# Token sums kept in spent raw tokens, an early ring, earlier weight sums and wider attention steps in an attention + MoE-style FFN kernel

## The chip, the cores and the metric

The kernel runs on one NeuronCore of one Trainium2 chip. Its engines work side by side, each with its own queue of instructions: TensorE (PE in the profile, PEld for its weight loads), VectorE (DVE), ScalarE (ACT), GpSimd (POOL) and SyncE (SP), which here issues all DMAs. The metric is the time of one execution in device microseconds (us).

## The reference

Windowed attention over 8 batches, 8 heads, 576 positions, head size 64, in fp32, and a feed-forward layer on its output. Heads 0 to 3 look back 32 positions, heads 4 to 7 look back 128 positions in steps of 4.

```python
scores = scale * q @ k.T                         # per batch and head
scores = np.where(mask, scores, -1e9); attn = softmax(scores); x = attn @ v
x = x.transpose(0, 2, 1, 3).reshape(4608, 512)   # tokens x d_model
h = x @ w_in                                     # 512 -> 2048
g = np.maximum(h, 0) + alpha * np.minimum(h, 0)
return g @ w_out                                 # 2048 -> 512
```

## The kernel before, in words

Every fp32 matrix is split into a high part (rounded to the fast fp32r type by ScalarE) and a low part (the rest, subtracted by VectorE). A product is three passes: high x high, high x low, low x high.

*Attention* works on 32 pairs of heads (class `Pair`; pair p is batch p // 4, heads 2c and 2c + 1 with c = p % 4). A pair has these steps: `scores` (72 small matmuls, L192), `maxima` (VectorE adds the mask and takes row maxima from PSUM, L216), `exponentials` (ScalarE, L228), `divisions` (VectorE, L235 to L238), `transposes` (TensorE, L248), `copies` (ScalarE, L255), `values` (72 small matmuls, L266), `highs` (ScalarE, L302) and `lows` (VectorE, L307 and L309), which put the result into token tiles. Tokens of the first three tiles of 512 go to split `x` tiles, later ones to unsplit *raw* tiles (`raw_xA0`, `raw_xB0`, `raw_xB1`, which share buffers with spent `x` tiles).

*The feed-forward layer* has two phases. In the first, three token tiles go through 48 *slices*, each one tile times 128 of the 2048 hidden columns: `ffn_h` (12 matmuls, L375), the activation (`ffn_sum`, or `ffn_parts` on VectorE, L396 and L397), `ffn_high` (ScalarE, L402), `ffn_low` (VectorE, L407), `ffn_y` (12 matmuls, L422). Slice n issues h of slice n + 1 and y of slice n - 1. The order of slices is tile 0's first eight, tile 1's sixteen, tile 0's last eight (24 to 31), tile 2's (32 to 47). When tile 0 resumes, its first partial output is loaded back from DRAM (`part`, L420) and added (L430).

The second phase (`paired_stage`) takes tiles 3 to 8 two at a time, in three stages with a Strassen-like scheme: seven products (`B11`, `B21`, `B22`, `T1` to `T4`) instead of eight. It needs sums of tokens (`token_parts`: T1 = z0 - k0, T2 = z1 - T1, T3 = z1 - z0, T4 = k1 - T2, where k0, k1 are the halves of the even raw tile, z0, z1 of the odd one) and sums of weights. Weights are saved to DRAM during slices 24 to 39 (`save`); in the last sixteen slices GpSimd forms sums for eight pairs of weight columns (`combine`, L465 and L468), ScalarE and VectorE split them (`split_combined`, L473 and L474), and they go to DRAM too. The stage reads all weights through a ring of ten buffers (`slot`, `take`, `feed`, L508).

Each stage has two groups; a group is an h part (`phase_h`, products of L561) and a y part (`phase_y`, L699) of four columns with eight *units* of six matmuls. Work of other kinds is hung on units by number (`hooks`): the steps of 12 attention pairs (`attention_hooks`: begin = scores, maxima, exponentials; middle = divisions, transposes, copies; end = values, highs, lows), and the token sums of the next stage. At the end of a column its result is copied to `py` (L717, L719) or added to it and stored (L722, L723).

The order on every engine is the program's order: the schedule is written out by hand (`manual_schedule`), and an engine that waits holds everything behind it. `score_at`, `turn_at`, `value_at` and `divide_at` say in which slice a pair takes its steps; `late_ops` holds the token sums of the first stage. `const.tile` with a tag that is in use waits until the earlier tile's readers are done. PSUM's four `a` banks are handed out in turn to h, scores, transposes and values.

Of the kernel before, what the change touches and what calls it, by code (L numbers as in the profile page):

```python
# [9 lines left out]
F32 = mybir.dt.float32  # L10
# [5 lines left out]
P = 128  # L16
# [17 lines left out]
EARLY = 21  # L34
# [23 lines left out]
def tile_window_attention_prelu_ffn(  # L58
# [381 lines left out]
    WBLOCK = {1: 0, 2: 1, 4: 2, 5: 3, 6: 4, 7: 5, 3: 6}  # L440
# [17 lines left out]
    def combine(i):  # L458

        if "t" not in sums_at:  # L460
            sums_at["t"] = const.tile([P, 8, 2 * P], F32, tag="xA1", name="wsum")
        t = sums_at["t"]
# [4 lines left out]
        for out, x, y, op in ((4, 2, 3, ALU.add), (5, 4, 0, ALU.subtract), (6, 0, 2, ALU.subtract), (7, 1, 5, ALU.subtract)):  # L467
            nc.gpsimd.tensor_tensor(out=t[:, out], in0=t[:, x], in1=t[:, y], op=op)  # L468

    def split_combined(i):  # L470
        t = sums_at["t"][:, 4:]
        hi, lo = (gbuf([P, 4, 2 * P], F32R, f"wc{i}_{a}") for a in range(2))
        nc.scalar.copy(out=hi, in_=t)  # L473
        nc.vector.tensor_tensor(out=lo, in0=t, in1=hi.bitcast(F32), op=ALU.subtract)  # L474
        for a, w in enumerate((hi, lo)):
            nc.sync.dma_start(out=wS[i, 3:7, :, a].rearrange("q p n -> p q n"), in_=w.bitcast(F32))

# [55 lines left out]
    def token_parts(t, tmp):  # L533
# [3 lines left out]
        T1, T2, T3, T4 = tmp  # L537
# [7 lines left out]
        def low(name, x):  # L545
# [4 lines left out]
        first = [diff(T1, z0, k0), high("T1", T1), low("T1", T1)]  # L550
        second = [
            diff(T2, z1, T1), high("T2", T2), diff(T3, z1, z0), high("T3", T3), low("T2", T2), low("T3", T3),
            diff(T4, k1, T2), high("B22", z1), high("T4", T4), low("B22", z1), low("T4", T4),
# [133 lines left out]
    def phase_y(t, grp, u, hooks):  # L687

        end = grp + 1 == NFP // GP
        for c in range(NC):  # L690
# [23 lines left out]
            for tt in range(2):  # L714
# [8 lines left out]
                nc.sync.dma_start(out=outT[c * P:(c + 1) * P, (t + tt) * TT:(t + tt + 1) * TT], in_=o)  # L723

    def attention_hooks(hooks, us, start, step):
        def put(n, *ops):
            hooks.setdefault(n, []).extend(ops)

        for k, u in enumerate(us):
# [24 lines left out]
            put(n + step + 1, end)  # L754

    def paired_stage():
# [3 lines left out]
        for t in range(NSTD, NTILE, 2):  # L760
            for grp in range(NFP // GP):
# [6 lines left out]
                attention_hooks(hooks, us, 2, 5)  # L768
                if grp and t + 2 < NTILE:
                    lots = token_parts(t + 2, [temporary(i) for i in range(1, 5)])  # L770
                    for at, lot in zip((4, 10, 20) if t == NSTD else (4, 10, 16), lots):
# [4 lines left out]
    held = {}  # L776

    def hold(i):
        if i not in held:
            held[i] = const.tile([P, 2 * TT], F32, tag=f"w{2 + i}_1", name=f"hold{i}")  # L780
        return held[i]

# [318 lines left out]
```

## Time and profile before

| | |
|---|---|
| time, median of 3 runs | 934.85 us (930.09 to 935.88) |
| profiled execution | 930.15 us; its span 928.4 us, granted TensorE clock 0.979 |
| busy time | PE 871.6 (94%), VectorE 554.2 (60%), ScalarE 426.0 (46%), GpSimd 55.7 (6%) |
| slices, first phase | to about 379 us |
| paired stages | from 385.5 us |
| bytes | 124.92 MB read from HBM, 33.55 MB written |

The profile is of one execution. Its timeline gives the start and length of instructions, with the idle time of the engine before and what ended it in brackets; its chain of waits follows the last work back to what released it; a table of stretches gives each engine's busy time between two moments. Line numbers (L508) are those of the kernel below. Matmuls overlap, so that a group's length is a little over the time that it adds.

### The profile page before, as it was taken

The page shows a single profiled execution, that of the slowest core. Times are in us where ns is not written, and L with a number is a line of the kernel's source. Part 1 is how long each engine was busy: PE and PEld are TensorE (multiplying, and loading weights), DVE is VectorE, ACT ScalarE, POOL GpSimd, SP SyncE. Part 2 cuts the span into 40 slices and gives each one's busy share as a digit, 9 for nine tenths or more (in the row PEclk, how much of TensorE's full clock was granted, in tenths as well). Part 3 has the DMA queues.
Part 4 walks back from the last instruction along what each step waited for, and adds up shares of the span by engine and source line. Part 5 has one row for each costly group of instructions (what it writes and reads, how often), then busy time and mean ns, then how long its engine had stood idle before and what let it go on. Part 6 is the DMA issues. An engine that isn't in the chain of part 4 may idle for free.

```text
span 928.4 us, 20670 instructions
## 1 busy us (share of the span) xinstructions
PE 871.6 (94%) x8080; PEld 710.5 (77%) x8080; DVE 554.2 (60%) x1607; ACT 426.0 (46%) x1250; POOL 55.7 (6%) x54
## 2 busy tenths in 40 slices
PE   4678999999989998799999989999999999999998
PEld 4467888878877876587788867887788888888886
DVE  6999587775667676576426755474337637503731
ACT  6776554554343443365535552455336316403610
POOL 0000000000305353100000000000000000000000
PEclk9879999999999999899999999999999999999999
DMA  9832153227879844675656646665456456535641
GB/s 338 295 126 70 46 191 111 68 78 230 254 241 315 269 156 133 234 240 149 189 174 191 185 145 191 190 184 167 116 159 184 143 156 201 150 95 157 184 135 47
DMA packets 101314, 159.83 MB, mean 172 GB/s; under 512 B 8416, under 2 KB 47456, under 8 KB 101216
## 3 DMA queue, kind: packets, MB, share of 16 engines
q1 hardware_dynamic: 101216, 158.51, 55.1%
q8 instruction: 64, 1.05, 0.5%
q14 instruction: 34, 0.28, 0.1%
HBM read 124.92 MB, written 33.55 MB: 171 GB/s over the span
## 4 chain that ended last, share of the span: by engine, by line
PE 54%; DVE 3%; ACT 2%; DMA 0%; issue 0%; ACTq 0%
PE y L699 26%; PE pA L561 14%; PE pC L561 7%; PE pB L561 4%; PE o L266 2%; ACT pr L228 1%; PE t L248 1%; PE s L192 1%; DVE gp L629 1%; DVE n L621 0%; DVE pr L238 0%; ACT n L617 0%; DMA ring_w<-wS 0%; DVE ob L722 0%; DVE stage L610 0%
## 5 line engine op out<-in xcount | busy, mean ns | idle before, releaser
L375 PE MATMUL h<-x,w_dt.float32r 128*128 128x512 f32 x576 | 145.6, 403 | 6.1 <-DVE nm L216 5.2
L422 PE MATMUL y<-g,w_dt.float32r 128*128 128x512 f32 x576 | 141.3, 395 | 1.8 <-DVE ob L430 1.8
L375 PEld LDWEIGHTS h<-x,w_dt.float32r 128*128 128x128 f32 x576 | 109.9, 194 | 30.5 <-issue 5.9
L422 PEld LDWEIGHTS y<-g,w_dt.float32r 128*128 128x128 f32 x576 | 107.6, 189 | 25.0 <-DVE ob L430 2.1
L699 PE MATMUL y<-gp,ring_w 128*128 128x512 f32 x480 | 114.7, 393 | 0.0
L699 PE MATMUL y<-gp,ring_xA 128*128 128x512 f32 x444 | 107.9, 396 | 0.0
L699 PEld LDWEIGHTS y<-gp,ring_w 128*128 128x128 f32 x480 | 89.0, 188 | 18.6
L228 ACT ACTIVATE pr<-pr,nm 128x64 f32<-128x64 f32 (+1 forms) x240 | 80.1, 335 | 36.2 <-DVE nm L216 36.2
L699 PEld LDWEIGHTS y<-gp,ring_xA 128*128 128x128 f32 x444 | 83.1, 190 | 17.4
L603 ACT COPY stage<-pA 128x512 f32<-128x512 f32 x72 | 42.3, 587 | 108.4 <-PE pA L561 108.2
L216 DVE CUSTOM_DVE_ANT_0 pr<-s,mask_sb 128x64 f32<-128x64 f32 (+1 forms) x288 | 45.0, 213 | 46.3 <-PE s L192 45.6
L402 ACT CAST g<-m 128x512 fp32r<-128x512 f32 x48 | 29.8, 621 | 84.9 <-DVE m L397 80.6
L561 PE MATMUL pA<-parts_w,ring_w 128*128 128x512 f32 x234 | 59.0, 396 | 6.9 <-DMA ring_w<-wS 6.9
L629 DVE TENSOR_TENSOR gp<-n,gp 128x512 fp32r<-128x512 f32 x96 | 63.1, 684 | 0.0
L621 DVE SCALAR_TENSOR_TENSOR n<-n,bal,stage 128x512 f32<-128x512 f32 x72 | 53.9, 749 | 13.9 <-ACT n L617 13.2
L625 ACT CAST gp<-n 128x512 fp32r<-128x512 f32 x96 | 56.6, 615 | 1.9 <-DVE n L621 1.9
L561 PEld LDWEIGHTS pA<-parts_w,ring_w 128*128 128x128 f32 x234 | 44.6, 191 | 16.5 <-issue 7.2
L561 PE MATMUL pA<-parts_w,ring_xA 128*128 128x512 f32 x228 | 56.1, 389 | 0.0
L699 PE MATMUL y<-gp,ring_g 128*128 128x512 f32 x228 | 55.5, 393 | 0.0
L617 ACT ACTIVATE n<-stage 128x512 f32<-128x512 f32 x72 | 45.6, 633 | 12.5 <-DVE stage L610 12.0
L722 DVE TENSOR_TENSOR ob<-y,py 128x512 f32<-128x512 f32 x24 | 16.4, 691 | 58.5 <-PE y L699 58.5
L561 PEld LDWEIGHTS pA<-parts_w,ring_xA 128*128 128x128 f32 x228 | 42.8, 188 | 8.9
(108 smaller groups left out, 1225.1 us busy)
## 6 DMA issues: line engine op xcount, KB each, us to landing
ring_w<-wS SPq DMA_DIRECT2D x68, 256.0 KB, 2.9
ring_xA<-wS SPq DMA_DIRECT2D x67, 256.0 KB, 2.9
v<-vW SPq DMA_DIRECT2D x24, 576.0 KB, 4.0
ring_w<-wO SPq DMA_DIRECT2D x40, 256.0 KB, 2.8
ring_xA<-wO SPq DMA_DIRECT2D x37, 256.0 KB, 2.8
out<-ob SPq DMA_DIRECT2D x36, 256.0 KB, 3.2
ring_g<-wS SPq DMA_DIRECT2D x33, 256.0 KB, 2.8
wO<-w_dt.float32r SPq DMA_DIRECT2D x32, 256.0 KB, 5.0
```

The source lines that it names most:

```text
L216: nc.vector.tensor_tensor_reduce(out=self.pr[rows, r, :], in0=self.ps[e][rows, g, :], in1=mask_sb[rows, kind, :], scale=-SCALE, scalar=3.0 ...
L228: nc.scalar.activation(out=self.pr[rows, r, :], in_=self.pr[rows, r, :], func=AF.Exp, bias=self.nm[rows, r:r + 1], scale=-1.0, accum_out=s ...
L375: nc.tensor.matmul(ms[t, f], lhsT=weight(0, a, f)[:, c * P:(c + 1) * P], rhs=half(t, c)[:, e, :], start=(c == 0 and n == 0), stop=(c == NC ...
L402: nc.scalar.copy(out=g[:, 0, :], in_=ms[t, f])
L422: nc.tensor.matmul(ys[t][c], lhsT=weight(1, a, f)[:, c * P:(c + 1) * P], rhs=g[:, e, :], start=(first and n == 0), stop=(last and n == 2),)
L561: nc.tensor.matmul(to, lhsT=w[:, (2 * a + c) * P:(2 * a + c + 1) * P], rhs=part_of(name, e)[:, c * TT:(c + 1) * TT], start=start and c == ...
L603: nc.scalar.copy(out=self.s(n), in_=self.A)
L617: nc.scalar.activation(out=self.m[n], in_=self.at(n), func=AF.Relu, scale=-1.0)
L621: nc.vector.scalar_tensor_tensor(out=self.m[n], in0=self.m[n], scalar=bal[:, f:f + 1], in1=self.at(n), op0=ALU.mult, op1=ALU.add)
L625: nc.scalar.copy(out=self.g(n)[:, 0], in_=self.m[n])
L629: nc.vector.tensor_tensor(out=g[:, 1], in0=self.m.pop(n), in1=g[:, 0].bitcast(F32), op=ALU.subtract)
L699: nc.tensor.matmul(ys2[tt], lhsT=w[:, k * P:(k + 1) * P], rhs=g[:, e], start=j == 0 and n == 0, stop=j == GF - 1 and n == 2)
```

## The change

- `token_parts` needs no temporary tiles: each difference is written over a raw token that is no longer needed (T1 and then T2 over k0, T3 over z0, T4 over k1), and T3 is formed before T2. The `hold` tiles of the first stage are gone.
- Eight of the ten fills of the ring are issued one per slice, in slices 40 to 47, instead of all after slice 47.
- `combine` runs at slices 25, 27, 31, 33, ..., 41 (before: 32, 34, ..., 46); the split comes two slices later and in two places, the rounding after `ffn_y` and the subtraction behind the values. The first two sums use another buffer; the sum tile has five rows instead of eight, with the blocks in another order (`WBLOCK`).
- The pairs 8 to 19 take their steps one slice earlier (`EARLY` 20), pair 8's values excepted, which stay in slice 23 and get a place of their own there.
- The token parts of the first stage: B11 in slice 39 (before 41), B21 and T1 in slice 43 (before 42 and 43), the rest in slices 45 to 47 as before.
- In the paired stages successive pairs begin 6 units apart (7 where four pairs share a group) instead of 5, the middle comes one unit before the next begin and the end with it; work of a unit beyond the last runs after the last. The token sums hang on other units.

```diff
-EARLY = 21
+EARLY = 20
...
-    WBLOCK = {1: 0, 2: 1, 4: 2, 5: 3, 6: 4, 7: 5, 3: 6}
+    WBLOCK = {1: 0, 2: 1, 4: 2, 3: 3, 7: 4, 5: 5, 6: 6}
...
-    def combine(i):
-        if "t" not in sums_at:
-            sums_at["t"] = const.tile([P, 8, 2 * P], F32, tag="xA1", name="wsum")
-        t = sums_at["t"]
+    def combine(i, tag):
+        if tag not in sums_at:
+            sums_at.clear()
+            sums_at[tag] = const.tile([P, 5, 2 * P], F32, tag=tag, name=f"wsum_{tag}")
+        t = sums_at[tag]
...
-        for out, x, y, op in ((4, 2, 3, ALU.add), (5, 4, 0, ALU.subtract), (6, 0, 2, ALU.subtract), (7, 1, 5, ALU.subtract)):
+        for out, x, y, op in ((3, 2, 3, ALU.add), (4, 3, 0, ALU.subtract), (2, 0, 2, ALU.subtract), (1, 1, 4, ALU.subtract)):
...
-    def split_combined(i):
+    def combined_high(i):
+        t, = sums_at.values()
+        wc[i] = [gbuf([P, 4, 2 * P], F32R, f"wc{i}_{a}") for a in range(2)]
+        nc.scalar.copy(out=wc[i][0], in_=t[:, 1:])
+
+    def combined_low(i):
+        t, = sums_at.values()
+        hi, lo = wc.pop(i)
+        nc.vector.tensor_tensor(out=lo, in0=t[:, 1:], in1=hi.bitcast(F32), op=ALU.subtract)
...
-        first = [diff(T1, z0, k0), high("T1", T1), low("T1", T1)]
+        first = [diff(k0, z0, k0), high("T1", k0), low("T1", k0)]
         second = [
-            diff(T2, z1, T1), high("T2", T2), diff(T3, z1, z0), high("T3", T3), low("T2", T2), low("T3", T3),
-            diff(T4, k1, T2), high("B22", z1), high("T4", T4), low("B22", z1), low("T4", T4),
+            diff(z0, z1, z0), high("T3", z0), diff(k0, z1, k0), high("T2", k0), low("T3", z0),
+            diff(k1, k1, k0), low("T2", k0), high("B22", z1), high("T4", k1), low("B22", z1), low("T4", k1),
         ]
...
+        for op in hooks.get(GF * NC, ()):
+            op()
...
         def put(n, *ops):
-            hooks.setdefault(n, []).extend(ops)
+            hooks.setdefault(min(n, GF * NC), []).extend(ops)
...
-            put(n + step + 1, end)
+            put(n + step, end)
...
-                attention_hooks(hooks, us, 2, 5)
+                if us:
+                    attention_hooks(hooks, us, *{5: (2, 6), 4: (3, 7), 3: (3, 6)}[len(us)])
                 if grp and t + 2 < NTILE:
-                    lots = token_parts(t + 2, [temporary(i) for i in range(1, 5)])
-                    for at, lot in zip((4, 10, 20) if t == NSTD else (4, 10, 16), lots):
+                    lots = token_parts(t + 2)
+                    for at, lot in zip((7, 16, 22) if t == NSTD else (5, 11, 14), lots):
...
-        zeroth, first, second = token_parts(NSTD, [hold(0), hold(1), hold(0), hold(0)])
-        late_ops[NS - 7], late_ops[NS - 6] = zeroth[:2], zeroth[2:]
-        late_ops[NS - 5] = first
-        late_ops[NS - 3], late_ops[NS - 2], late_ops[NS - 1] = second[:4], second[4:8], second[8:]
+        zeroth, first, second = token_parts(NSTD)
+        late_ops[NS - 9] = zeroth[:2]
+        late_ops[NS - 5] = zeroth[2:] + first
+        late_ops[NS - 3], late_ops[NS - 2], late_ops[NS - 1] = second[:5], second[5:8], second[8:]
...
-        turn_at[n + 2] = value_at[n + 2] = pairs[p]
+        turn_at[n + 2] = pairs[p]
+        value_at[n + 3 if p == 2 * NC else n + 2] = pairs[p]
...
+    split_at, combine_at = {}, {}
+    for k in range(NFP):
+        n = SECOND + 1 + 2 * k + (2 if k > 1 else 0)
+        combine_at[n] = (k + NFP // 2) % NFP
+        split_at[n + 2] = combine_at[n]
...
+        if valued is pairs[2 * NC]:
+            valued.values()
+            valued.highs()
+            valued.lows()
         if turned:
             turned.transposes()
             turned.copies()
         if not whole:
             ffn_y(*slices[n - 1])
+        if n in split_at:
+            combined_high(split_at[n])
         if scored:
             scored.scores()
-        if valued:
+        if valued and valued is not pairs[2 * NC]:
             valued.values()
+        if n in split_at:
+            combined_low(split_at[n])
         if scored:
             scored.maxima()
...
-        if n >= SECOND + CUT:
-            k = n - SECOND - CUT
-            i = (k // 2 + NFP // 2) % NFP
-            if k % 2 == 0:
-                combine(i)
-            else:
-                split_combined(i)
-        if n == NS - 7:
+        if n in combine_at:
+            combine(combine_at[n], "xB1" if n < SECOND + 5 else "xA1")
+        if n == NS - 9:
             plan_parts()
         for op in late_ops.pop(n, ()):
             op()
-
-    for _ in range(NRING - 2):
-        feed()
+        if n >= NS - NRING + 2:
+            feed()
+
     ffn_y(*slices[-1])
     feed()
     feed()
```

More of the change, by code (lines that the diff above doesn't have):

```diff
@@ L466, in combine @@
                 out=t[:, 2 * j:2 * j + 2].rearrange("p q n -> p (q n)"), in0=hi, in1=lo, op=ALU.add)
-        for out, x, y, op in ((4, 2, 3, ALU.add), (5, 4, 0, ALU.subtract), (6, 0, 2, ALU.subtract), (7, 1, 5, ALU.subtract)):
+        for out, x, y, op in ((3, 2, 3, ALU.add), (4, 3, 0, ALU.subtract), (2, 0, 2, ALU.subtract), (1, 1, 4, ALU.subtract)):
             nc.gpsimd.tensor_tensor(out=t[:, out], in0=t[:, x], in1=t[:, y], op=op)
-    def split_combined(i):
[L471 to L474, printed above, removed]
+    def combined_high(i):
[6 more added lines that the diff above has]
+        nc.vector.tensor_tensor(out=lo, in0=t[:, 1:], in1=hi.bitcast(F32), op=ALU.subtract)
         for a, w in enumerate((hi, lo)):
             nc.sync.dma_start(out=wS[i, 3:7, :, a].rearrange("q p n -> p q n"), in_=w.bitcast(F32))
+    wc = {}
     PRODUCTS = (1, 7, 6, 2, 5, 3, 4)
@@ L531, in small, with token_parts @@
         return temporary(1 + i % 8 // 2)[:, i % 2 * TT:(i % 2 + 1) * TT]
-    def token_parts(t, tmp):
+    def token_parts(t):
         k0, k1, z0, z1 = raw(t, 0), raw(t, 1), raw(t + 1, 0), raw(t + 1, 1)
-        T1, T2, T3, T4 = tmp
         def diff(out, x, y):
@@ L774, in paired_stage @@
                 phase_y(t, grp, last, hooks)
[L776 to L781, printed above, removed]
     late_ops = {}
     def plan_parts():
-        zeroth, first, second = token_parts(NSTD, [hold(0), hold(1), hold(0), hold(0)])
-        late_ops[NS - 7], late_ops[NS - 6] = zeroth[:2], zeroth[2:]
-        late_ops[NS - 5] = first
-        late_ops[NS - 3], late_ops[NS - 2], late_ops[NS - 1] = second[:4], second[4:8], second[8:]
+        zeroth, first, second = token_parts(NSTD)
+        late_ops[NS - 9] = zeroth[:2]
+        late_ops[NS - 5] = zeroth[2:] + first
+        late_ops[NS - 3], late_ops[NS - 2], late_ops[NS - 1] = second[:5], second[5:8], second[8:]
     slices = [(0, f) for f in range(CUT)] + [(1, f) for f in range(NF)] + [(0, f) for f in range(CUT, NF)]
@@ L1013, in tile_window_attention_prelu_ffn @@
             scored.exponentials(0, 5)
-        if valued:
+        if valued and valued is not pairs[2 * NC]:
             valued.highs()
@@ L1020, in tile_window_attention_prelu_ffn @@
             if u is pairs[2 * NC]:
-                due = n == CUT + 4, n == CUT + 4
+                due = n == CUT + 3, n == CUT + 3
             else:
```

## The prediction

> **What bounds the kernel now.** I read the busy slices first, then the table of stretches, the gaps in TensorE's timeline, and the chain of waits. From 100 us on TensorE (PE) is busy in nearly every slice, so time can only come out of its gaps. I cut the stretch that the change touches at the first value matmul (L266) or score matmul (L192) of a pair, and at the end of the last slice. Columns: stretch, length, busy time (instructions) of PE, its weight loads, VectorE, ScalarE and GpSimd, granted clock, DMA share, GB/s:
>
> ```profile
> 186.51:214.94 28.43, 27.81 (x396) 22.32 (x395) 21.13 (x81) 13.06 (x54) 0.00 (x0) 1.00 0.39 130
> 228.74:242.52 13.78, 13.78 (x203) 11.39 (x197) 8.40 (x37) 6.06 (x27) 0.00 (x0) 1.00 0.70 220
> 242.52:274.06 31.54, 28.77 (x401) 23.24 (x394) 20.31 (x77) 11.39 (x52) 8.88 (x8) 1.00 0.72 234
> 274.06:331.53 57.47, 56.34 (x789) 45.46 (x789) 40.42 (x148) 26.57 (x108) 25.56 (x24) 1.00 0.88 281
> 331.53:346.70 15.17, 14.44 (x204) 11.48 (x198) 11.51 (x38) 8.29 (x29) 8.38 (x6) 1.00 0.42 149
> 346.70:366.15 19.45, 14.85 (x130) 11.76 (x125) 13.59 (x40) 7.87 (x29) 7.61 (x6) 0.91 0.35 116
> 366.15:378.65 12.50, 12.50 (x121) 10.00 (x120) 9.52 (x11) 6.16 (x8) 4.60 (x4) 1.00 0.47 151
> 378.65:388.41 9.76, 2.90 (x8) 2.35 (x8) 5.30 (x6) 2.02 (x3) 0.00 (x0) 0.65 0.70 225
> ```
>
> Two slices with one pair cost 13.78 us when nothing disturbs them (row 228.74, PE never idle). By that yardstick 2 x 13.78 were due in 242.52:274.06 (loss 4.0), 4 x 13.78 in 274.06:331.53 (2.3), 13.78 in 331.53:346.70 (1.4) and again in 346.70:366.15 (5.7). The units of PE work, from the chain of waits (start, length, what):
>
> ```profile
> 432.18 3.44 ACT pr L228 x20
> 439.07 0.91 PE s L192 x56
> 441.57 1.18 PE o L266 x72
> 539.66 2.52 PE y L699 x6
> 883.83 40.81 PE y L699 x180
> ```
>
> 40.81 / 180 is 0.227 us a matmul: 1.36 for six (one hook unit of the paired stages), 2.72 for twelve (half a slice). A pair's transposes cost 13.78 - 4 x 2.72 - 0.91 - 1.18 = 0.8. In 366.15:378.65 were due 4 x 2.72 + 1.18 = 12.06: loss 0.4. In the last stretch one product of 1.36 was due: loss 8.4.
>
> **The ring, filled during the last slices.** The 8.4 us in the timeline (start, length, engine, line; in brackets the idle time before and its releaser):
>
> ```profile
> 381.53 1.22 DVE L546 TENSOR_TENSOR parts_w<-hold,parts_w 128x1024 fp32r<-128x1024 f32 x1
> 382.78 1.76 SPq L508 DMA_DIRECT2D ring_w<-wS  x4
> 385.51 2.90 PE L561 MATMUL pA<-parts_w,ring_w 128*128 128x512 f32 x6 [6.86 <-DMA ring_w<-wS]
> ```
>
> The ring shares buffers with the `hold` temporaries, so the first fill starts when VectorE has read the last of them (381.53 + 1.22 = 382.75); then come the landing and six matmuls at half clock. Token sums in their own raw tokens free these buffers, and eight fills go out one per slice from slice 40. The first product needs B11, made in slice 39. So 8.4 goes to 0. Next late are the last token parts: B22's low and T4 are used by the seventh and eighth product, 8 us after the first, with two VectorE steps of 1.22 ahead of them: hidden. The two fills of g0 stay where they were.
>
> **Weight sums from slice 25.** The same eight sums, so what counts is what runs beside them:
>
> ```profile
> 263.36 0.16 DVE L235 TENSOR_SCALAR rs<-sums 128x10 f32<-128x10 f32 x1
> 263.81 0.89 DVE L238 TENSOR_TENSOR pr<-pr,rs 128x512 f32<-128x512 f32 x2
> 295.06 3.39 POOL L468 TENSOR_TENSOR wsum<-wsum 128x256 f32<-128x256 f32 x4 [7.85 <-DVE wc L474]
> 296.93 1.66 DVE L238 TENSOR_TENSOR pr<-pr,rs 128x512 f32<-128x512 f32 x2
> 299.12 0.73 DVE L396 TENSOR_SCALAR m<-h,al 128x512 f32<-128x512 f32 x1
> ```
>
> A division takes 1.3 (263.36 to 264.70); under GpSimd's sums its products take 1.66 instead of 0.89, and the transposes wait. After, a sum starts at the end of an odd slice, when that slice's division is over, and is done before the next one. The 2.3 and the 1.4 go, and so does the 0.4 (slice 47 has no split any more). Under the sums now lie the maxima (L216), which the trace never shows there: at least 0; at most they wait until the sum ends (first rival). I take 0, by the nearest row: L396, which like them reads PSUM, keeps 0.73.
>
> [...]
>
> **Slices 43 to 45** lose the 5.7:
>
> ```profile
> 352.12 1.23 DVE L474 TENSOR_TENSOR wc<-wsum,wc 128x1024 fp32r<-128x1024 f32 x1 [2.48 <-ACT wc L473]
> 353.27 1.22 DVE L540 TENSOR_TENSOR hold<-raw_xB,raw_xB 128x1024 f32<-128x1024 f32 x1
> 354.52 1.05 ACT L543 CAST parts_w<-hold 128x1024 fp32r<-128x1024 f32 x1 [2.43 <-DVE hold L540]
> 356.91 0.74 DVE L396 TENSOR_SCALAR m<-h,al 128x512 f32<-128x512 f32 x1
> 360.29 0.41 PE L248 MATMUL t<-ident,pr 128*128 128x128 f32 x2 [3.74 <-DVE pr L238]
> 361.94 0.73 DVE L396 TENSOR_SCALAR m<-h,al 128x512 f32<-128x512 f32 x1
> 362.08 4.14 PE L422 MATMUL y<-g,w_dt.float32r 128*128 128x512 f32 x12
> 364.03 0.69 ACT L255 COPY pt<-t 128x320 f32<-128x320 f32 x2
> ```
>
> VectorE sat behind ScalarE's rounding of the weight sum, then did T1, so the next activation (356.91) and division came late. After, pair 19 is a slice earlier, but slice 43 carries more: division, the last weight split, B21's low, T1's difference and low. Let 0 be the end of slice 43's h matmuls. ScalarE's rounding of the sum needs the buffer of y's operand, so it ends at 2.72 + 1.05 and VectorE's split at 5.0 (activation, division and low are done by 3.4). Steps of 1.22 and 1.05: B21's low ends at 6.3, T1's difference at 7.5, its rounding at 8.6, its low at 9.8. Only then follow the next activation, its rounding and, behind that on ScalarE, pair 19's copies: 2.8 (361.94 to 364.72), so 12.6. PE is ready for pair 19's values at 3 x 2.72 + 0.8 = 9.0. The stall moves from the transposes of slice 45 to the values of slice 44: 3.6, and as now 1.4 for the halved clock (4.14 - 2.72). 5.0 for 5.7: gain 0.7; bounds of the new stall 2 (VectorE overlaps its steps) and 6.5 (as late as 356.91 now).
>
> Every long gap is followed by a slow stretch here: 2.90 for six matmuls behind 6.86 us, 4.14 for twelve behind 3.74. [...]
>
> **Slices 29 to 33** lose 4.0, mostly to this:
>
> ```profile
> 259.02 0.35 SPq L188 DMA_DIRECT2D v<-vW  x1
> 263.53 2.46 SPq L420 DMA_DIRECT2D ob<-part  x4
> 268.99 2.66 DVE L430 TENSOR_TENSOR ob<-y,ob 128x512 f32<-128x512 f32 x4 [3.70 <-DMA ob<-part]
> ```
>
> The adds start 5.5 us after the loads of the first partials are issued, and y's banks wait. With the pairs a slice earlier, slice 32 has these adds *and* scores: its maxima queue behind the adds, and h of slice 34 needs the bank that the maxima free. Let 0 be the end of slice 30's scores. SyncE issues v at 1.2, needs 4.5 to pass k, q and four saves (259.02 to 263.53) and about 2.5 for the four saves of slice 31, so the loads go out at 8.2. The adds run from 13.7 to 16.4, the first six maxima end about 1 later; PE wants the bank at 1.18 + 4 x 2.72 + 2.9 (a pair's 0.8 + 0.91 + 1.18) = 15.0. Stall 2.4 (0 if SyncE is 2.4 us quicker, 5 if as much slower): gain 1.6.
>
> **Pair 8 at slice 20.** VectorE still converts weights there:
>
> ```profile
> 189.49 0.75 DVE L389 SCALAR_TENSOR_TENSOR m<-m,nal,h 128x512 f32<-128x512 f32 x1
> 194.49 0.69 DVE L397 SCALAR_TENSOR_TENSOR m<-h,m 128x512 f32<-128x512 f32 x1
> ```
>
> Slice 22's run up to the release of its h bank is 5.7 us (189.49 to 195.18). After, slice 21 hands over late: its low waits for 3.44 us of exponentials and a rounding, then come the low, the division and two conversion steps, about 7.5 from the end of pair 8's scores. So the bank is free at 13.2, and pair 9's scores, which take it, are due at 4 x 2.72 + 0.8 = 11.7. Stall 1.5, and I put 0.6 on the next banks and on slice 24, where stores and scores meet. 2.1 against 28.43 - 27.56 = 0.9 now: loss 1.2 (bounds 0 and 3).
>
> **Paired stages.** Every gap there is a transpose waiting for a division:
>
> ```profile
> 436.94 0.73 PE L248 MATMUL t<-ident,pr 128*128 128x128 f32 x5 [1.05 <-DVE pr L238]
> 457.71 0.79 PE L248 MATMUL t<-ident,pr 128*128 128x128 f32 x5 [0.70 <-DVE pr L238]
> 538.47 1.19 PE L248 MATMUL t<-ident,pr 128*128 128x128 f32 x5 [3.12 <-DVE pr L238]
> 561.01 0.74 PE L248 MATMUL t<-ident,pr 128*128 128x128 f32 x5 [0.57 <-DVE pr L238]
> 633.39 0.74 PE L248 MATMUL t<-ident,pr 128*128 128x128 f32 x5 [1.04 <-DVE pr L238]
> 654.13 0.74 PE L248 MATMUL t<-ident,pr 128*128 128x128 f32 x5 [0.70 <-DVE pr L238]
> ```
>
> They sum to 7.2, and the half clock after 538.47 adds (2.52 - 1.36) + (1.19 - 0.74) = 1.6: 8.8. The middle step moves from four units after the scores to five or six, which covers 1.05, 1.04 and, with the token steps behind the division, 3.12. The others stand where a division in unit 16 queues behind the copies or adds at a column's end. After, that happens in unit 8 of tile 3, group 1 (0.6) and unit 16 of tile 5 (0.7). Two more pairs of group 1 have a token rounding behind their 3.44 us of exponentials and VectorE's low behind that (3.44 + 0.4 + 1.05 + 1.22 + 1.3 = 7.4 against 5 x 1.36): 0.6, and 1.4 where adds and T1's difference come first. And tile 3's fifth pair ends after the last unit: its values wait for the copies (0.5), the next product for the bank that they fill (1.0). Sum 4.8, gain 4.0 (bounds 0 and 8). Values one unit after the transposes fit: copies 0.7, unit 1.36.
>
> **Sum.** 8.4 + 2.3 + 1.4 + 0.4 + 0.7 + 1.6 - 1.2 + 4.0 = 17.6. The profiled execution took 930.15 us (span 928.4): 912.6. The runs shown lie between 930.09 and 935.88, their median 4.7 above the profiled one, which is at the fast end; for the median I add half of that: **915**.
>
> **Rivals.**
> *Maxima held by the sums (slower).* If an instruction that reads the mask waits for GpSimd as the division does, the maxima end with the sum. A sum starts about 0.4 before the even slice's h ends and h of the next slice wants the bank 5.6 after it: a sum of 6.4 (25.56 / 4) plus 0.9 of maxima costs 1.3, one of 8.4 (331.53) 3.3; from 2.2 each nothing is gained. Eight at 3.3 are 26: 939, as a median 941. Against it stands the 0.73 of L396.
> *The stalls only move.* With the new stalls at their upper bounds (slice 44 6.5, slice 33 5, early loss 3, paired gain 0) 17.6 - 1.5 - 2.6 - 1.8 - 4.0 = 7.7 is left: 922, as a median up to 927. For it: VectorE's queue is full in slice 43.
> *The fills are held.* SyncE issues in order, and the fills stand behind weight splits and loads that wait for PE. If the first is late, the 8.4 stays: 921 to 924. Against it: the first four buffers are free by slice 34.
> *Both new stalls stay away.* If slices 33 and 44 hide them, 5.0 + 2.4 more go: 905.
>
> **How the numbers follow.** Forecast 0.55, stalls only move 0.16, both away 0.15, fills held 0.06, maxima held 0.06, no effect at all 0.02. A difference of 1% (9.3 us of 934.85) is about what a measurement tells from none. Faster by more: the forecast, "both away" and nearly half of the next two, 0.80; within: 0.14; slower: 0.06. The range from 904 to 926 leaves out the slow rival and the tails.
>
> **What will show it.** PE's L561 begins right behind the last L422, with no gap before a DMA; transposes wait under 0.2 in slices 34 to 42; a gap of 2 to 5 us stands before L266 in slice 44, ended by L255's copies; one ended by L216 stands before L375 in slice 33. It is wrong if L216 lengthens under L465 and L468, or if the ring's first landing is still a releaser.

## The result, and the profile after

| | before | after |
|---|---|---|
| time, median of 4 runs each, side by side | 933.85 us (930.09 to 935.88) | 919.04 us (918.59 to 921.12) |
| ratio, with its 95% interval | | 0.985 (0.9814 to 0.9887) |
| profiled execution, span | 930.15 us, 928.4 us | 919.12 us, 917.3 us |

The changed kernel is 1.5% faster. The forecast was 915 us, with 904 to 926 as its range: the direction and the range hold, but the sum behind it was 17.6 us and the two traces show 13. (The profiled times differ by 11.0, because the after execution reached the changed part 2.07 us later, by instructions that are the same in both: pair 8's scores start at 183.14 after and, a slice of 5.44 us later in the program, at 186.51 before. So 13.1 belongs to the change; the terms below give 13.0.)

The table of stretches of the changed kernel, cut as in the prediction at a pair's first score or value matmul. Columns as there: stretch, length, busy time of PE, its weight loads, VectorE, ScalarE and GpSimd, granted clock, DMA share, GB/s.

```profile
183.14:217.15 34.01, 29.31 (x395) 23.61 (x394) 26.70 (x85) 15.24 (x58) 7.08 (x6) 0.95 0.18 54
258.52:290.30 31.78, 29.73 (x400) 24.08 (x395) 19.23 (x77) 12.07 (x51) 6.67 (x8) 0.95 0.94 298
290.30:345.47 55.17, 55.17 (x794) 45.57 (x788) 37.42 (x147) 27.82 (x109) 23.16 (x24) 1.00 0.87 275
345.47:361.85 16.38, 12.95 (x133) 10.58 (x126) 12.22 (x40) 8.55 (x29) 1.54 (x3) 0.99 0.52 169
361.85:382.56 20.71, 20.71 (x145) 17.28 (x145) 12.92 (x16) 7.32 (x11) 0.00 (x0) 0.85 0.25 88
```

Eight slices in 290.30:345.47 now run without any idle time of PE: 55.17 is four times 13.79. The other rows hold what is still lost. Their causes are in PE's timeline (start, length, what, idle time before and its releaser):

```profile
200.75 1.30 PE L192 MATMUL s<-k,q 64*32 64x64 f32 x70 [4.70 <-DVE m L397]
276.12 4.58 PE L375 MATMUL h<-x,w_dt.float32r 128*128 128x512 f32 x12 [1.84 <-DVE nm L216]
361.85 2.41 PE L266 MATMUL o<-pt,v 64*64 64x32 f32 x72 [3.43 <-ACT pt L255]
364.19 4.91 PE L375 MATMUL h<-x,w_dt.float32r 128*128 128x512 f32 x12
...
374.40 8.32 PE L422 MATMUL y<-g,w_dt.float32r 128*128 128x512 f32 x36
382.56 0.62 PE L567 MATMUL pA<-parts_w,ring_w 128*128 128x512 f32 x2
...
448.90 7.10 PE L705 MATMUL y<-gp,ring_xA 128*128 128x512 f32 x30 [0.99 <-issue]
533.36 0.74 PE L248 MATMUL t<-ident,pr 128*128 128x128 f32 x5 [0.57 <-DVE pr L238]
556.91 0.74 PE L248 MATMUL t<-ident,pr 128*128 128x128 f32 x5 [0.90 <-DVE pr L238]
639.99 0.74 PE L248 MATMUL t<-ident,pr 128*128 128x128 f32 x5 [0.70 <-DVE pr L238]
```

(L567, L705 and L515 are the L561, L699 and L508 of before; GpSimd's L466 and L469 are L465 and L468; VectorE's L479, L546 and L552 are L474, L540 and L546.) The first product stands directly behind the last y: the 6.86 us wait for the ring is gone. Three stalls are left in the slices: 4.70 us in slice 22, 1.84 in slice 33, 3.43 in slice 44, each with a stretch at half clock behind it: the granted clock is 0.50 from 201.01 to 204.42, from 276.11 to 279.52 and from 361.44 to 368.27 us. An h of twelve matmuls reads 3.0 in this view when nothing slows it, here 4.58 and 4.91.

Against the terms of the prediction (us lost against an undisturbed TensorE; two slices with one pair 13.78 us each):

| term | lost before | forecast for after | after | gain forecast | gain |
|---|---|---|---|---|---|
| ring | 8.4 | 0 | 0 | 8.4 | 8.4 |
| eight steady slices, and the two behind them | 2.3 + 1.4 | 0 | 0 | 3.7 | 3.7 |
| slices 43 to 45, and the last ones | 5.7 + 0.4 | 5.0 | 6.6 | 1.1 | -0.5 |
| slices 29 to 33 | 4.0 | 2.4 | 4.2 | 1.6 | -0.2 |
| slices 20 to 24 | 0.9 | 2.1 | 6.4 | -1.2 | -5.5 |
| paired stages | | | | 4.0 | 7.1 |
| sum | | | | 17.6 | 13.0 |

The ring and the steady slices came out as forecast. Three stalls of VectorE's queue cost nearly 8 us more than forecast, and the paired stages gave 3 us more.

### The profile page after: what moved, and what is told of

The parts are those of the page before. It is cut to its first block, busy times and chain, and to the rows that moved or that the text cites. A ratio compares the mean times of both kernels' runs of the same rounds, so it can differ in the third digit from the quotient of the medians.

```text
span 917.3 us, 20648 instructions
## 1 busy us (share of the span) xinstructions
PE 869.6 (95%) x8080; PEld 714.5 (78%) x8080; DVE 549.4 (60%) x1607; ACT 428.1 (47%) x1250; POOL 48.8 (5%) x54
## 3 DMA queue, kind: packets, MB, share of 16 engines
q8 instruction: 64, 1.05, 0.5%
## 4 chain that ended last, share of the span: by engine, by line
PE 87%; DVE 7%; ACT 2%; DMA 1%; issue 1%; SPq 1%; DVEq 0%; ACTq 0%
PE y L705 28%; PE pA L567 14%; PE h L375 14%; PE y L422 13%; PE pC L567 7%; PE pB L567 4%; PE o L266 3%; PE s L192 3%; PE t L248 2%; DMA ws<-w_in 1%; ACT w_dt.float L228 1%; DVE w_dt.float L216 1%; DVE w_dt.float32r L363 1%; DVE wa L352 0%; DMA w_dt.uint<-w_out 0%
## 5 line engine op out<-in xcount | busy, mean ns | idle before, releaser
L375 PE MATMUL h<-x,w_dt.float32r 128*128 128x512 f32 x576 | 150.7, 414 | 7.3 <-DVE nm L216 6.9
L375 PEld LDWEIGHTS h<-x,w_dt.float32r 128*128 128x128 f32 x576 | 114.2, 201 | 33.0 <-issue 7.3
L705 PE MATMUL y<-gp,ring_w 128*128 128x512 f32 x480 | 113.7, 392 | 0.0
L705 PE MATMUL y<-gp,ring_xA 128*128 128x512 f32 x444 | 104.7, 391 | 1.0 <-issue 1.0
L705 PEld LDWEIGHTS y<-gp,ring_w 128*128 128x128 f32 x480 | 89.3, 188 | 18.6
L705 PEld LDWEIGHTS y<-gp,ring_xA 128*128 128x128 f32 x444 | 82.8, 188 | 18.4 <-issue 1.1
L627 DVE SCALAR_TENSOR_TENSOR n<-n,bal,stage 128x512 f32<-128x512 f32 x72 | 53.9, 749 | 13.9 <-ACT n L623 13.1
L567 PE MATMUL pA<-parts_w,ring_w 128*128 128x512 f32 x234 | 57.7, 390 | 0.0
L567 PE MATMUL pA<-parts_w,ring_xA 128*128 128x512 f32 x228 | 56.2, 390 | 0.5 <-ACT raw_xB L302 0.5
L705 PE MATMUL y<-gp,ring_g 128*128 128x512 f32 x228 | 55.0, 393 | 0.0
L567 PEld LDWEIGHTS pA<-parts_w,ring_w 128*128 128x128 f32 x234 | 43.8, 188 | 9.1
L567 PEld LDWEIGHTS pA<-parts_w,ring_xA 128*128 128x128 f32 x228 | 42.7, 188 | 9.5 <-ACT raw_xB L302 0.6
```

Of the source, the lines that this page charges most:

```text
L375: nc.tensor.matmul(ms[t, f], lhsT=weight(0, a, f)[:, c * P:(c + 1) * P], rhs=half(t, c)[:, e, :], start=(c == 0 and n == 0), stop=(c == NC ...
L567: nc.tensor.matmul(to, lhsT=w[:, (2 * a + c) * P:(2 * a + c + 1) * P], rhs=part_of(name, e)[:, c * TT:(c + 1) * TT], start=start and c == ...
L627: nc.vector.scalar_tensor_tensor(out=self.m[n], in0=self.m[n], scalar=bal[:, f:f + 1], in1=self.at(n), op0=ALU.mult, op1=ALU.add)
L705: nc.tensor.matmul(ys2[tt], lhsT=w[:, k * P:(k + 1) * P], rhs=g[:, e], start=j == 0 and n == 0, stop=j == GF - 1 and n == 2)
```

## The experiments

None of these kernels leaves out a part of the computation. Where an experiment was run once, its time stands beside the kernel before on the same chip (933.12 us, one run, for the kernels of slices 22, 33 and 44 and for the one with the fills behind the loop) and the reading goes by its trace.

### Slice 22: GpSimd's first sum starts early

GpSimd has nothing queued ahead of the first `combine`, which the program issues in slice 25. It starts as soon as its buffer is free, which is in slice 22. VectorE's and GpSimd's timeline of the changed kernel there:

```profile
192.66 2.98 POOL L466 TENSOR_TENSOR wsum_xB<-w_dt.float32r 128x512 f32<-128x512 f32 x2 [191.36 <-PE t L248]
...
192.97 1.52 DVE L348 TENSOR_SCALAR wa<-wa 128x512 f32<-128x512 f32 x1
194.53 1.39 DVE L350 TENSOR_SCALAR wa<-wa 128x512 uint32<-128x512 uint32 x1
```

L348 and L350 convert weights; their usual length is 0.42. The experiment holds the sum back with an addition that needs g of slice 26:

```diff
+        if n == SECOND + 1:
+            gate = const.tile([P, 5, 2 * P], F32, tag="xB1", name="wsum_xB1")
+            sums_at["xB1"] = gate
+            late_x = gs[slices[n + 1]][:, 1, :2 * P].bitcast(F32)
+            nc.gpsimd.tensor_tensor(out=gate[:, 0], in0=late_x, in1=late_x, op=ALU.add)
         if n in combine_at:
```

> The changed kernel with one more GpSimd addition (128 x 256, its result is not used) that reads the low part of g of slice 26 and writes the buffer of the first weight sum. GpSimd therefore starts the first sum in slice 25 instead of at 192.66 us, in slice 22. Theory (GpSimd's sum holds VectorE's weight conversions, and this is the stall of slice 22): L348 and L350 of those slices take 0.42 us again instead of up to 1.5, the gap of 4.70 us before the scores of slice 22 falls to 1 to 1.6 us (the 1.5 that was forecast for VectorE's own load), and the half clock behind it goes (another 1.3): 4 to 4.5 us less between 183 and 217 us, by the same cut. Rival (VectorE's own load makes the stall, GpSimd only runs beside it): the gap stays at 4 us or more.

It ran in 911.92 us, 7.2 below the changed kernel's profiled time. Timeline and stretch of this run:

```profile
193.91 0.42 DVE L348 TENSOR_SCALAR wa<-wa 128x512 f32<-128x512 f32 x1
...
198.16 0.95 PE L192 MATMUL s<-k,q 64*32 64x64 f32 x70 [1.18 <-DVE m L397]
...
221.63 2.52 POOL L466 TENSOR_TENSOR wsum_xB<-w_dt.float32r 128x512 f32<-128x512 f32 x2
```

```profile
184.07:213.20 29.13, 27.88 (x395) 22.49 (x395) 23.07 (x85) 15.26 (x58) 0.00 (x0) 1.00 0.21 63
```

The stretch falls from 34.01 to 29.13, by 4.9 us, and L348 takes 0.42. What is left of the gap, 1.18, is VectorE's own load, forecast at 1.5. So GpSimd's sum is shown to be the cause of the rest; the rival falls. Five steps of VectorE account for it: beside the sum L348 and L350 lose 2.1 us, and the three steps with two SBUF inputs behind them (L407, L352 and L354, 1.21, 1.21 and 1.09 instead of 0.69) 1.4, together the 3.5 between 4.70 and 1.18. Another 2.9 us came further on, nearly all from the clock: the waits in slices 33 and 44 have nearly the same length here (1.66 and 3.43), but less half clock behind them (31.78 fell to 30.11 and 20.71 to 19.44, the latter at a granted clock of 0.91 instead of 0.85).

### Slice 44: VectorE's queue in slice 43

```diff
-        late_ops[NS - 5] = zeroth[2:] + first
+        late_ops[NS - 7] = zeroth[2:]
+        late_ops[NS - 4] = first
```

> The changed kernel with the two lots of token steps of slice 43 set apart: B21's low in slice 41, T1's difference, rounding and low in slice 44. Theory (VectorE's queue in slice 43 makes the stall before the values of slice 44): the gap of 3.43 us before L266 and the half clock of the h behind it (two windows, about 3.1 us) go, and the stretch from the values of slice 42 to those of slice 44 (16.38) and the next one (20.71) lose 6.5 us together. Rival (the late ScalarE rounding of the weight sum alone holds VectorE): about 2 us of gap stay, and half of the slow clock. Second rival (T1 so late only moves the stall to slice 45 or to the first products): the same 6.5 us turn up further on.

It ran in 912.05 us. VectorE's timeline of the changed kernel shows the queue that the edit takes apart, and the table of stretches of the edited one what comes of it:

```profile
353.59 1.23 DVE L479 TENSOR_TENSOR wc<-wsum_xA,wc 128x1024 fp32r<-128x1024 f32 x1 [0.55 <-ACT wc L474]
354.73 1.22 DVE L552 TENSOR_TENSOR parts_w<-raw_xB,parts_w 128x1024 fp32r<-128x1024 f32 x1
355.86 1.22 DVE L546 TENSOR_TENSOR raw_xB<-raw_xB,raw_xB 128x1024 f32<-128x1024 f32 x1
...
358.20 1.22 DVE L552 TENSOR_TENSOR parts_w<-raw_xB,parts_w 128x1024 fp32r<-128x1024 f32 x1 [1.12 <-ACT parts_w L549]
359.35 0.74 DVE L396 TENSOR_SCALAR m<-h,al 128x512 f32<-128x512 f32 x1
```

```profile
345.01:357.88 12.87, 12.87 (x132) 10.57 (x126) 9.15 (x37) 6.77 (x27) 2.35 (x4) 1.00 0.63 207
357.88:375.51 17.63, 17.63 (x145) 14.76 (x145) 13.65 (x16) 8.00 (x11) 0.00 (x0) 1.00 0.29 101
```

After the split of the weight sum (353.59) come three token steps, and only then the activation (359.35) on which ScalarE's copies for the values wait. With B21's low two slices earlier and T1 a slice later the two stretches take 12.87 and 17.63 instead of 16.38 and 20.71: 3.5 of gap and 3.1 of half clock (0.50 from 361.44 to 368.27 in the changed kernel, twice 3.41 us; the second stretch is at 1.00 here and at 0.85 there), 6.6 together, and PE is busy all the time. Both rivals fall: the split alone leaves no gap, and nothing turns up later.

### Slice 33: the additions ahead of the maxima

```diff
+        adds = []
         if not whole:
-            ffn_y(*slices[n - 1])
+            ffn_y(*slices[n - 1], later=adds)
...
         if scored:
             scored.maxima()
+        for op in adds:
+            op()
+        if scored:
             scored.exponentials(0, 5)
```

(`ffn_y` now puts the additions of L430 and their output DMAs into `adds` instead of issuing them; that part of the edit is not shown.)

> The changed kernel with the four additions to the partial outputs of tile 0 (L430) and their four output DMAs issued after the maxima of slice 32 instead of ahead of them. Theory (the maxima stand behind the additions in VectorE's queue, and the bank that they free is late): the gap of 1.84 us before h (L375, ended by L216) and the 1.6 us of half clock go, 3.4 us in all. Rival (the additions hold y's banks, which are then late): the gap moves to y or to the next scores and at least 2 us stay.

It ran in 920.44 us: nothing gained. In the changed kernel the additions start at the end of y, and the maxima stand behind them:

```profile
272.27 2.85 DVE L430 TENSOR_TENSOR ob<-y,ob 128x512 f32<-128x512 f32 x4
275.04 0.21 DVE L216 CUSTOM_DVE_ANT_0 pr<-s,mask_sb 128x64 f32<-128x64 f32 x1
```

The edit does take that wait away (values to values 13.78 us, before it 17.27), but the next two slices take 17.93 instead of 13.81. PE's timeline, and the DMA queues' packets in 288 to 289 us (packets, MB, share of 16 engines):

```profile
288.03 1.00 PE L266 MATMUL o<-pt,v 64*64 64x32 f32 x50
291.38 0.86 PE L266 MATMUL o<-pt,v 64*64 64x32 f32 x22 [2.35 <-issue]
292.18 4.19 PE L375 MATMUL h<-x,w_dt.float32r 128*128 128x512 f32 x12
```

```profile
q1 hardware_dynamic: 377, 0.38, 109.3%
q8 instruction: 1, 0.02, 5.8%
```

PE stops after 50 of 72 matmuls, at 289.03, and the rest wait for no engine. Just before, between 288.9 and 289.0, a packet of instructions starts through DMA queues that are full; PE goes on 2.4 us later. In the changed kernel the packet of this place came in 285 to 286 us, four to five before the same values (290.30). So neither theory nor rival: the three and a half microseconds were gained, and a new wait took them back.

### The three together, and the new wait

First all three edits, the gate on the first sum, the split lots of slice 43 and the additions behind the maxima:

> The three edits together: the first weight sum held until slice 25, T1 a slice later and B21's low two slices earlier, the additions to the partial outputs behind the maxima of slice 32. Theory (three separate stalls of VectorE's queue): the gains of the three add up, 4 to 4.5 + 6.5 + 3.4, so about 905 us against 919. Rival (what one stall hides, the next one takes): under 7 us, 912 or more.

The median is 906.43 us (904.66 to 907.88), 0.9715 of before (0.9691 to 0.9739). The total of the theory came, though its terms did not: the third gave nothing, the clock behind the first gave more. The same 2.27 us stop stands inside the values of slice 33, again behind 50 of 72. Then the first two edits alone, and all three with the stores of tile 0 out of the way:

> The first two edits without the third: the first weight sum held until slice 25, T1 a slice later and B21's low two slices earlier; the additions to the partial outputs as in the changed kernel. In the run with the additions alone moved, the wait of the maxima went, but 2.35 us before the values of the next slices came in its place, with a half clock behind, so that nothing was gained. Theory (the third edit earns nothing in company either): the gap before h (L375) is back with 1.6 to 1.8 us, no gap stands in the values behind it, and the time is within 1.5 us of the three edits' 906.4. Rival (the third edit is worth its 3.4 us here): 908.5 or more.

> All three edits, and the four output DMAs of tile 0 issued at the end of slice 40, when the weights have been saved, instead of in slice 32. Theory (the gap of 2.27 us inside the values of slice 33, which no engine releases, is TensorE waiting for its next block of instructions, which stands behind the data in the DMA queues): with 1 MB less ahead of it the block comes about 3 us earlier, the gap goes, and the stretch from the values of slice 33 to those of slice 34 takes 13.8 instead of 16.34 us: 904 against 906.4. Rival (the instruction block is limited by something else than the DMA traffic, or the gap has another cause): a gap of 2 us or more stays at the same place, 906 to 907.

The last kernel's edit, against all three:

```diff
                 def add(c=c):
                     nc.vector.tensor_tensor(out=o[c], in0=ys[t][c], in1=o[c], op=ALU.add)
-                    nc.sync.dma_start(out=outT[c * P:(c + 1) * P, t * TT:(t + 1) * TT], in_=o[c])
+                def store(c=c):
+                    nc.sync.dma_start(out=outT[c * P:(c + 1) * P, t * TT:(t + 1) * TT], in_=o[c])
+                late_stores.append(store)
...
+        if n == SECOND + NF:
+            for op in late_stores:
+                op()
```

Both ran side by side: two edits 908.02 us (906.49 to 908.23), ratio 0.9733 (0.9716 to 0.9749); three edits with late stores 904.09 us (902.92 to 905.01), ratio 0.9694 (0.9678 to 0.9711). With two edits the wait of the maxima is back, and is as dear as the stop that the third edit put in its place (16.39 us for the stretch, 16.34 with three). With the stores in slice 40 the stop of 2.27 us is gone and the stretch of the values is clean, with PE busy all the time (table of stretches):

```profile
281.35:295.16 13.81, 13.81 (x205) 11.40 (x198) 9.14 (x37) 6.75 (x27) 5.81 (x7) 1.00 0.97 303
```

The packet of instructions comes in 278 to 279 us, over two microseconds ahead of these values. So with 1 MB of stores moved the stop does not come: that this stop hangs on the stores is shown; that this one packet is what PE waits for is argued from its time and from the same place in both runs. The two edits lie 1.6 us above the three by medians of different chips, a little more than the 1.5 expected, and under the rival's 908.5. The last kernel is the fastest of all: 29 us below before on its chip, where the changed kernel was 15 below before on its own.

### The ring: what had held it

Two kernels ask which edit freed the ring. The changed kernel with the eight fills back behind the loop:

```diff
-        if n >= NS - NRING + 2:
-            feed()
+    for _ in range(NRING - 2):
+        feed()
```

> The changed kernel with the eight ring fills back behind the loop, where they were before. Theory (the ring's stall was made by the late readers of the buffers, the temporaries, and not by the place of the fills): SyncE's last wait for other work is in slice 44, so that the fills go out soon after it and the first product still stands behind the last y without a gap: 0 to 0.5 us lost. Rival (the place of the fills was what mattered): 6 to 8.4 us of gap before the first product, ended by the first landing.

919.36 us, as the changed kernel. SyncE's issues and PE's timeline:

```profile
365.33 1.85 SPq L515 DMA_DIRECT2D ring_w<-wS  x4
...
383.11 1.52 PE L567 MATMUL pA<-parts_w,ring_w 128*128 128x512 f32 x6
```

The fills go out 17.8 us ahead of the first product, although they are issued last. Then the kernel before with nothing but token sums in spent tokens (T3 formed over z0, T2 and T1 over k0, T4 over k1, no `hold` tiles):

```diff
-        first = [diff(T1, z0, k0), high("T1", T1), low("T1", T1)]
+        first = [diff(k0, z0, k0), high("T1", k0), low("T1", k0)]
...
-        zeroth, first, second = token_parts(NSTD, [hold(0), hold(1), hold(0), hold(0)])
+        zeroth, first, second = token_parts(NSTD)
```

> The kernel before with the token sums formed in the spent raw tokens, and nothing else: no temporaries, everything else and the place of the fills as before. Theory (two things held the ring: the temporaries' readers, and behind them the last weight split of slice 47, whose DMA stands ahead of the fills in SyncE's queue): the gap of 6.86 us before the first product falls by 2 to 5 us only, since the fills go out at 379 to 381 us instead of 382.8. Rival (the temporaries alone): the gap falls under 1 us and all 8.4 us come back.

It ran in 933.34 us beside a median of 932.55 for before. SyncE, VectorE and PE:

```profile
373.67 11.74 SPq L476 DMA_DIRECT2D wS<-wc  x4
...
383.81 1.21 DVE L474 TENSOR_TENSOR wc<-wsum,wc 128x1024 fp32r<-128x1024 f32 x1
...
385.46 2.49 SPq L508 DMA_DIRECT2D ring_w<-wS  x4
...
389.07 2.48 PE L560 MATMUL pA<-parts_w,ring_w 128*128 128x512 f32 x5 [5.75 <-DMA ring_w<-wS]
```

The gap falls only from 6.86 to 5.75. The fills stand behind the DMA of the last weight split, which ends at 385.02 (383.81 + 1.21). Counted from the start of the last y's (374.86 here, 370.19 before) the split ends where it did, after 10.2 us (before 10.3), but now it is what the fills wait for: the first goes out after 10.6 us instead of 12.6. Of these 2.0 us 0.9 are lost again, since the first product starts 3.6 us behind the first fill instead of 2.7; why was not tried. The theory's mechanism holds, its size does not (2 to 5 expected, 1.1 measured). Two holders in series, then: taking away one shows the other.

### The paired stages

The changed kernel with the old spacing of the attention steps:

```diff
-            put(n + step, end)
+            put(n + step + 1, end)
...
-                    attention_hooks(hooks, us, *{5: (2, 6), 4: (3, 7), 3: (3, 6)}[len(us)])
+                    attention_hooks(hooks, us, 2, 5)
...
-                    for at, lot in zip((7, 16, 22) if t == NSTD else (5, 11, 14), lots):
+                    for at, lot in zip((4, 10, 20) if t == NSTD else (4, 10, 16), lots):
```

> The changed kernel with the paired stages' schedule of before: pairs 5 units apart, middle 4 units after the scores, end one unit behind the next pair's scores, and the old units for the token sums. By the traces of before and after the four groups with attention lost 7.1 us (1.0, 4.2, 1.9 and 0): theory, all of it comes back, to groups of about 99.6, 97.0, 96.2 and 81.6 us. Rival, the forecast's term: 4.0 us come back, and the other 3.1 belong to something else that changed (the ring's earlier start, the token sums without temporaries).

923.63 us. The groups that hold attention, from the second product of one to that of the next; first the kernel before (292.82 us together), then the changed kernel, then this one:

```profile
388.21:487.81 99.60, 97.85 (x1106) 79.04 (x1105) 50.37 (x195) 49.58 (x168) 0.00 (x0) 1.00 0.65 198
487.81:584.81 97.00, 93.18 (x809) 75.39 (x808) 58.34 (x152) 45.60 (x123) 0.00 (x0) 0.98 0.59 173
584.81:681.03 96.22, 94.48 (x957) 76.64 (x956) 46.86 (x166) 45.16 (x144) 0.00 (x0) 1.00 0.56 163
```

```profile
383.92:482.50 98.58, 96.76 (x1106) 79.70 (x1105) 50.73 (x196) 50.02 (x168) 0.00 (x0) 1.00 0.61 189
482.50:575.26 92.76, 91.20 (x809) 74.41 (x807) 57.63 (x152) 45.93 (x123) 0.00 (x0) 1.00 0.61 182
575.26:669.61 94.35, 93.65 (x957) 76.95 (x956) 47.52 (x167) 45.60 (x144) 0.00 (x0) 1.00 0.57 169
```

```profile
382.96:482.44 99.48, 97.73 (x1107) 78.92 (x1105) 50.50 (x196) 49.61 (x168) 0.00 (x0) 1.00 0.61 188
482.44:577.86 95.42, 91.59 (x809) 74.25 (x808) 58.26 (x152) 45.55 (x123) 0.00 (x0) 1.00 0.58 176
577.86:674.15 96.29, 94.54 (x958) 76.63 (x956) 46.84 (x166) 45.20 (x144) 0.00 (x0) 1.00 0.55 163
```

285.69 against 291.19: the spacing is worth 5.5, between theory (7.1) and rival (4.0). The other 1.6 is the half clock behind the gap of 3.12 (0.50 from 538.60 to 542.00 in the kernel before). That gap is back here, but the transposes behind it take 0.74, not 1.19 as in the kernel before, and the group's granted clock is 1.00, there 0.98: a gap of the same length without the half clock, so these 1.6 are no merit of the spacing. Of the 5.5 the gaps make 3.2: they sum to 7.2 here (1.05, 0.70, 3.12, 0.57, 1.05, 0.70), to 4.0 in the changed kernel (0.99, 0.30, 0.54, 0.57, 0.90, 0.70). What is the rest?

```diff
-            put(n + step - 1, middle)
-            put(n + step, end)
+            put(n + step - 1 - ahead, middle)
+            put(n + step - ahead, end)
...
-                    attention_hooks(hooks, us, *{5: (2, 6), 4: (3, 7), 3: (3, 6)}[len(us)])
+                    attention_hooks(hooks, us, *{5: (2, 6), 4: (3, 7, 1), 3: (3, 6)}[len(us)])
```

> The changed kernel with middle and end of the four pairs of tile 5, group 0, one unit earlier (their start stays), so that the values of a pair stand in the unit ahead of the next pair's scores and no longer in the same one. Theory (values and scores side by side save about 0.28 us a pair, since TensorE changes between kinds of work less often): the group grows from 94.35 to 95.2 us or more, gaps before transposes taken off. Rival (the gain is only in the gaps before the transposes): the group's time changes by the change of its gaps and by nothing else, under 0.3 us.

```profile
576.67:671.70 95.03, 94.33 (x957) 76.72 (x956) 47.52 (x167) 45.58 (x144) 0.00 (x0) 1.00 0.55 165
```

The run took 921.22 us. The group grew from 94.35 to 95.03 with the same gap of 0.70 in it: 0.17 us for each of four pairs, not the 0.28 expected, and more than the rival's 0.3 in all. Twelve pairs make 2.0, near the 2.3 that were open.

## Why the prediction was right, and where it was wrong

**The ring (8.4, right in size, half right in reason).** The prediction gave two reasons: spent tokens free the buffers, and the fills go out one per slice. The fills' place is worth nothing here, and the spent tokens alone free 1.1 us of gap. What was missing is the last weight split ahead of the fills in SyncE's queue. The change moved that too, out of slice 47, and with both holders gone the whole 8.4 came; the split moved alone was not tried. The prediction spoke of the order of SyncE's queue only as a rival.

**The steady slices (2.3 + 1.4, right).** A division's cost fell as forecast, and the first rival, maxima held by the sums, is refuted. The group of division products before and in the changed kernel (busy us, mean ns | idle before), and from the changed kernel's timeline a sum with the maxima under its tail:

```profile
L238 DVE TENSOR_TENSOR pr<-pr,rs 128x512 f32<-128x512 f32 (+1 forms) x48 | 27.8, 621 | 0.8
```

```profile
L238 DVE TENSOR_TENSOR pr<-pr,rs 128x512 f32<-128x512 f32 (+1 forms) x48 | 21.3, 485 | 0.8
```

```profile
302.36 3.29 POOL L469 TENSOR_TENSOR wsum_xA<-wsum_xA 128x256 f32<-128x256 f32 x4
...
304.22 0.23 DVE L216 CUSTOM_DVE_ANT_0 pr<-s,mask_sb 128x64 f32<-128x64 f32 x1 [1.36 <-PE s L192]
```

The products took 27.8 us, now 21.3; a maximum beside the sum keeps 0.23.

**Pair 8 at slice 20 (the step that failed, -1.2 against -5.5).** The prediction costed VectorE's own run to the bank and got 1.5; without GpSimd the run shows 1.18. But it took the sums to begin "at the end of an odd slice", slice 25, from their place in the program. GpSimd, with an empty queue, started at 192.66 us, when the new buffer was free, three slices earlier. There the sum met the weight conversions, which no sum had met before. Beside it not only steps with two SBUF inputs grow: L348 and L350 have one, and took 1.52 and 1.39 instead of 0.42 and 0.43, where L396 of before, which reads PSUM, kept 0.73 beside a sum. What sets these steps apart was not tried.

**Slices 29 to 33 (a mis-sized term, 1.6 against -0.2).** The stall of slice 33 is the one described, the maxima behind the additions, 1.84 against 2.4. But its time came out right by luck: the loads of the partials went out 9.8 us after slice 30's scores (268.33), not 8.2, and the additions began 3.9 us behind them without a wait for a DMA, when y had ended (272.27), not 5.5, so that they started 13.75 us after these scores, where the prediction has 13.7. What was missing is the clock behind the stall: 4.58 instead of 3.0 for an h, at a granted clock of 0.50 from 276.11 to 279.52.

**Slices 43 to 45 (a mis-sized term, 0.7 against -0.9).** The chain came step by step as forecast; the gap, too (3.43 against 3.6). The clock was put at 1.4 and took 3.1 (20.71 against 17.63 without the gap).

**The paired stages (mis-sized, 4.0 against 7.1).** The forecast of what gaps remain was near, 4.8 against 4.0, and it named the places of five of the six; the largest, 0.99 without a releaser, it did not have, and one that it listed (0.6) stayed away. The 1.6 of the clock were in its sum and came. So 0.8 of the difference comes from the gaps, and 2.3 from what it did not list: nearly all of that, by the four pairs tried, from values and scores side by side.

**The time of the whole.** Half of the 4.7 us between the profiled execution and the median was added. The changed kernel's profiled execution is at its median (919.12, 919.04), and its runs spread over 2.5 us, not 5.8. From 930.15 less 13.0 comes 917.2; the 2.07 us of a later start are the rest. That the time lies so near the forecast is in part luck: without the 2.3 us of the paired stages that the sum did not have, it would have been 921.

## What to carry to other kernels

An operation's place in the program need not say when it starts: GpSimd, with nothing queued, began a sum of slice 25 in slice 22, at 192.66 us. On an idle engine look for the last reader of the operation's buffer, and price what it meets there (here 3.5 us of gap). When two things hold the same resource in series, removing one alone can show little (6.86 us of gap fell to 5.75), so follow the queue past the first releaser before crediting an edit. And after a stall is removed, look for what takes its place: here the maxima's wait went, and a stop of 2.3 us inside the values came, until 1 MB of stores was moved.

## What the runs showed of the hardware that was not expected

**The half clock did not go by a gap's length alone.** A gap of 1.84 us in slice 33 was followed by an h of 4.58; one of 1.66 and one of 2.55 at the same place, in other runs, by h at 2.97 and 3.00:

```profile
272.12 2.97 PE L375 MATMUL h<-x,w_dt.float32r 128*128 128x512 f32 x12 [1.66 <-DVE nm L216]
```

```profile
273.08 3.00 PE L375 MATMUL h<-x,w_dt.float32r 128*128 128x512 f32 x12 [2.55 <-DVE nm L216]
```

(The first is of the run with the first sum held, the second of the run with two edits.) The 3.43 us in slice 44 cost 3.1 of slow clock in the changed kernel and 1.8 in the run with the first sum held (20.71 and 19.44 against 17.63, at granted clocks of 0.85, 0.91 and 1.00).

In the changed kernel the slow stretches behind the three stalls, 201.01 to 204.42, 276.11 to 279.52 and 361.44 to 368.27, are 3.41 us long or twice that, with a granted clock of 0.50 in them and 1.00 on both sides. Their starts lie 75.10 and 85.33 us apart, within 0.1 of 22 and 25 times 3.41. The second begins as the gap of 1.84 us ends (276.12). What sets where such a stretch begins, and why the 2.55 us of the other run had none behind them, was not shown.

**Stops of TensorE that no engine ended stood 2.2 to 2.6 us behind packets of instructions.** The page of the changed kernel counts 64 packets on queue q8 (instruction), 1.05 MB, and 16,160 matmuls and weight loads: by an estimate from these counts some 250 to a packet, if all are PE's. Scores and values are 288 of these instructions in about 2 us. In slice 33 with the additions moved, a packet started between 288.9 and 289.0 us, and PE stood from 289.03 to 291.38; with 1 MB of stores moved as well as all three edits in place, PE did not stop there. The traces of before and of the changed kernel have five idle times of PE of 0.2 us or more without a releaser behind the first 90 us: 1.13 us (until 91.18) and 0.40 (333.16) before, 1.41 (91.69), 0.21 (259.97) and 0.99 (448.90) in the changed kernel. All lie within or right behind scores and values, and each ends 2.2 to 2.6 us after a packet of q8 starts. The 0.99 us before 448.90 follow values and scores set side by side, and no idle time of that length is in this group with the old spacing (the group's 1.75 us are the 1.05 and 0.70 before transposes); the packet starts between 446.2 and 446.3. The DMA share is 0.31 from 446 to 449 us, against 109.3% on q1 alone at the stop in slice 33 (288 to 289 us). That PE waits there for its instructions is an estimate from these times; only the stores of slice 32 were tried.
